# The down projection by seven products instead of eight, in 16 blocks of a fused attention and MLP kernel

## The chip, the cores and the metric

The kernel runs on one core of one Trainium2 chip. The metric is the device time of one execution in microseconds (us). TensorE (PE) multiplies matrices into PSUM; VectorE (DVE), ScalarE (ACT) and GpSimd (POOL) do elementwise work; SyncE (SP) and ACT issue the transfers.

## The reference

One transformer layer for 2048 tokens of width 576: conditioned layer norm, attention over the last 512 keys of a cache with 32 query heads, and an MLP, each with a gated residual. What matters here is the MLP:

```python
gate = jnp.einsum("bsd,df->bsf", x, W_gate)       # 576 -> 4608
up = jnp.einsum("bsd,df->bsf", x, W_up)
gate = gate * (gate > 0)
h = gate * up
return jnp.einsum("bsf,fd->bsd", h, W_down)       # 4608 -> 576
...
h = _layernorm(x, axis=-1) * (1 + cb) + sb
x = x + gb * _B_ref(h, B_W_gate, B_W_up, B_W_down)
```

All is float32. The kernel gets near float32 accuracy from rounded operands: each operand is split into a high part (`hi`, a rounded copy made by ACT) and a low part (`lo`, the remainder, made by POOL's subtraction), and each product is computed as hi\*hi + hi\*lo + lo\*hi, three matmuls.

## The kernel before

The attention takes the first 1640 us or so. Then comes the MLP, in 36 blocks. Blocks m = 0 to 17 (`NFP` is 18) handle the first 1024 tokens, blocks 18 to 35 the second 1024. One block covers 256 of the 4608 hidden features (two tiles of 128, index f) and 1024 tokens (two halves of 512, index k).

Gate and up projection: a block's 2x2 arrangement (f, k) is computed by a seven-product (Strassen-Winograd) scheme. `order(m)` gives the seven slots P1, P6, P2, P7, P5, P4, P3. In each slot `prod` runs twice (xx = 0 gate, xx = 1 up), 7 matmuls of 512 columns each time, into a pair of PSUM banks `gu`; three such pairs rotate. `evac` then takes the result out: in P1 ACT copies it, in P6 and P7 DVE adds a 1024-wide tile, in P2, P5, P4 and P3 DVE finishes one of the four (f, k) tiles of h with two or three instructions (`gated`), and `h_out` splits it: ACT writes `hhi`, POOL writes `hlo`.

Down projection: while block m computes its gate and up products, `md_piece` computes the down product of block m - 1, one piece for each token tile of 128: 2 column halves x 2 feature tiles x 3 = 12 matmuls of 288 columns into the PSUM tile of pool `psW`, which has one buffer, and one DVE addition into the accumulator `acc[i]` in SBUF. `mlp_slots` places the eight pieces of a block among the half slots: slot 0 has one behind its second `prod`, slot 1 one behind each, slots 2 to 6 one behind the first. The last block's pieces follow at the end with nothing beside them; there they alternate between `psW` and `psS`.

The down weights: in blocks 0 to 17 each pair of 128 rows is loaded raw (`rogb`), multiplied by the gate row on DVE, split by ACT and POOL into `wogb`, used, and stored in its split form to memory (`dk`, 576 KB). In blocks 18 to 35 the split form is loaded again. The gate and up operands (`wop`, from `wk`, 640 KB each) and the normalised tokens (`hop`) are loaded again in the same way there.

The order on PE, DVE, ACT and POOL is the order of the program. SP's queue is ordered by the compiler's scheduler.

Of the kernel before, what the change touches and what calls it, by code (L numbers as in the profile page):

```python
# [25 lines left out]
H2 = D // 2  # L26
# [7 lines left out]
def kernel(  # L34
# [13 lines left out]
    nc = tc.nc  # L48
# [182 lines left out]
    mods = {}  # L231
# [183 lines left out]
    qhi, qlo, pthi, ptlo, ohi, olo = {}, {}, {}, {}, {}, {}  # L415
# [25 lines left out]
    st_, t4, t5, pt, hi_, lo_, bc, rb, rinv, ks_, pvps, done, o, bps = ({} for _ in range(14))  # L441
# [192 lines left out]
    NFP = NFT // 2  # L634
    NB = 2 * NFP
    ds_, hhi, hlo = {}, {}, {}
    wop, wraw, hop = {}, {}, {}
    pair, tmp = {}, {}

    def md_piece(m, k, qt, pool=None):  # L640
        b, fp = divmod(m, NFP)
        i = 8 * b + 4 * k + qt
        down_piece([hhi[m, f, k] for f in range(2)], [hlo[m, f, k] for f in range(2)],
                   [ds_[m, f] for f in range(2)], i, qt, f"md{m}_{k}_{qt}", pool=pool)()
        if fp == NFP - 1:
            nc.sync.dma_start(out[i * P:(i + 1) * P, :], acc[i])
# [5 lines left out]
    def order(m):  # L652
        return ("P1", "P6", "P2", "P7", "P5", "P4", "P3")
# [265 lines left out]
    def prod(m, s, n, xx):  # L919

        hs, w = hop[m // NFP, OPS[s][1]], wop[n]
        ps = pair[m, s][:, xx, :]
        ops = []
        for t in range(2):
            ops += [(w[:, xx, t, :], hs[t]), (w[:, xx, 3 + t, :], hs[t]), (w[:, xx, t, :], hs[3 + t])]
        ops.append((w[0:96, xx, 2, :], hs[2][0:96]))
        for i, (a, c) in enumerate(ops):
            nc.tensor.matmul(ps, a, c, start=s not in ("P2", "P3") and i == 0, stop=i == len(ops) - 1,  # L928
                             skip_group_check=True)

    HI = {(0, 0): (op, "ohi"), (1, 0): (op, "ohi"), (1, 1): (bp, "bc"), (0, 1): (bp, "bc")}

    def h_out(m, f, k, r):
        pool, tag = HI[f, k]
# [8 lines left out]
        nc.scalar.copy(hi, r)  # L943
        nc.gpsimd.tensor_sub(lo, r, hi.bitcast(F32))  # L944

    def gated(m, f, k, ps, r, a, op1=ALU.add):

        if a is None:
            nc.vector.tensor_scalar(r, ps[:, 0, :], 0.0, None, op0=ALU.max)
        else:  # L950
            nc.vector.tensor_tensor(r, ps[:, 0, :], a[:, 0, :], op=ALU.add)  # L951
            nc.vector.tensor_tensor(ps[:, 1, :], ps[:, 1, :], a[:, 1, :], op=op1)  # L952
        nc.vector.scalar_tensor_tensor(r, r, 0.0, ps[:, 1, :], op0=ALU.max, op1=ALU.mult)  # L953
        h_out(m, f, k, r)
# [9 lines left out]
    def new_pair(m, s):  # L964
        pair[m, s], kind[m, s] = new_banks(f"gu{npair[0]}")

    def evac(m, s):
        ps = pair[m, s]
        if s == "P1":
            t = tmp["q"] = pp.tile([P, 2, 512], F32, tag="hi", name=f"q{m}")  # L970
            nc.scalar.copy(t, ps)
        elif s == "P2":
            gated(m, 0, 0, ps, xp.tile([P, 640], F32, tag="xm", name=f"r{m}")[:, :512], None)
        elif s == "P6":
            nc.vector.tensor_tensor(tmp["q"], ps, tmp["q"], op=ALU.add)  # L975
        elif s == "P7":
            t = tmp["r"] = pp.tile([P, 2, 512], F32, tag="lo", name=f"r{m}", bufs=2)
            nc.vector.tensor_tensor(t, ps, tmp["q"], op=ALU.add)
            nc.scalar.copy(tmp["q"][:, 1, :], ps[:, 1, :])
        elif s == "P5":  # L980
            t = pp.tile([P, 2, 512], F32, tag="lo", name=f"c22_{m}", bufs=2)
            gated(m, 1, 1, ps, t[:, 0, :], tmp["r"])
        elif s == "P4":
            gated(m, 1, 0, ps, tmp["r"][:, 0, :], tmp["r"])
        else:

            gated(m, 0, 1, ps, tmp["q"][:, 0, :], tmp["q"], ALU.subtract)

    def wd_prep(m, f):
        tag = "wB" if f else "wC"  # L990
        k = 2 * (m % NFP) + f
        if m < NFP:
            load, gate, cut = prep_out(ds_, k, wd, "gb", (m, f), (None, tag))

            def keep():
                cut()
                stores.append((dkeep[k], ds_[m, f][2]))

            return load, gate, keep

        def back():
# [194 lines left out]
    for i, ab in enumerate(lay0 + lay):  # L1196
        n = i - len(lay0) - 2 * NFT + 4
# [4 lines left out]
    def mat(m, s, fn, sums=False):  # L1202
        mextra.setdefault((m, s, sums) if s < 6 else (m + 1, -1, sums), []).append(fn)

    for m in range(NB):
        for f in range(2):
            for k, fn in enumerate(wd_prep(m, f)):
                if m >= NFP:
                    at_ = m, 3 * f
                elif f and m:  # L1210
                    at_ = ((m - 1, 5), (m, 0), (m, 1))[k]
                else:
                    at_ = m, k + (k > 0 and m > 0) + 2 * f
                mat(*at_, fn, sums=k == 1)
# [25 lines left out]

    def mlp_slots():
        for m in range(NB):
            md = [lambda k=k, qt=qt: md_piece(m - 1, k, qt) for k in range(2) for qt in range(4)] if m else []
            for i, s in enumerate(order(m)):
                flush_stores()
                if s not in ("P2", "P3"):
                    new_pair(m, s)
                else:
                    pair[m, s], kind[m, s] = (x[m, {"P2": "P1", "P3": "P5"}[s]] for x in (pair, kind))
                prod(m, s, 7 * m + i, 0)  # L1250
                if m or i:
                    sums(m, i)
                    others(m, i)
                if m and i:
                    md.pop(0)()
                elif filler and not m:
                    filler.pop(0)()
                for fn in mextra.pop((m, i - 1, True), []):
                    fn()
                prod(m, s, 7 * m + i, 1)  # L1260
# [12 lines left out]
        flush_stores()  # L1273
        assert not mextra and not filler
# [204 lines left out]
```

## Time and profile before

| | us |
|---|---|
| median of the runs | 2948.91 |
| lowest and highest run | 2943.78 and 2950.67 |
| the profiled execution's own span | 2950.2 |
| its granted TensorE clock, mean | 0.994 |

The page gives no other time for the profiled execution than its span; it lies within the runs, 1.3 above their median. Of the span PE is busy 2880.4 us, DVE 2103.5, POOL 1870.3 and ACT 1364.6. In the page's groups, `L583` is the line of the down product's matmuls (`md`; the attention's output product shares it as `wo`), `L594` the addition into the accumulator, `L928` the gate and up matmuls (`gu`), `L943` and `L944` the two halves of `h_out`. A row of a timeline gives start, length, engine, line, operation, the tile written and those read, and in brackets the idle time of the engine before it and what ended it. A row of a group gives the count, the busy time, the mean length in ns, and the idle time before. A stretch gives the busy time of each engine in that part of the span, with the number of instructions, then the granted clock and the share of time that transfers filled.

### The profile page before, as it was taken

To read this page: it belongs to the slowest core of one execution; us is meant where nothing else is said; L and a number is where in the kernel's file an instruction comes from. 1 tells how busy PE (TensorE), PEld (TensorE's weight loads), DVE (VectorE), ACT (ScalarE), POOL (GpSimd) and SP (SyncE) were. 2 spreads that over 40 slices of the span, in tenths; PEclk is the share of its full clock that TensorE was granted. 3 is DMA by queue.
4 is the path that set the end of the run, shared out by engine and by line. 5 is a ranking of instruction groups with operands and counts; after the bars stand their busy time and mean duration, and the time that the engine had idled before them with its cause. 6 is when DMAs were issued, how large, how long until landed. Compare 5 with 4: busy or idle time off the path is not lost. (4 is left out here: it accounts for less than half of the span.)

```text
span 2950.2 us, 41160 instructions
## 1 busy us (share of the span) xinstructions
PE 2880.4 (98%) x15406; PEld 2514.2 (85%) x15406; DVE 2103.5 (71%) x2916; ACT 1364.6 (46%) x1869; POOL 1870.3 (63%) x1308
## 2 busy tenths in 40 slices
PE   6799999999999999999999999999999999999999
PEld 5688888888888888888888788888888888888888
DVE  7878888788888888777889676677677444444444
ACT  4466666666676666666656343333333111111110
POOL 5588888888888888777787667777777111111111
PEclk9899999999999999999999999999999999999999
DMA  4011222222323223322244477776777854555443
GB/s 149 22 44 54 82 93 84 67 96 95 98 86 100 92 66 128 101 68 83 70 142 142 138 253 252 267 268 254 264 259 282 285 166 161 168 174 167 158 166 112
DMA packets 167303, 424.75 MB, mean 144 GB/s; under 512 B 15424, under 2 KB 62272, under 8 KB 167104
## 3 DMA queue, kind: packets, MB, share of 16 engines
q1 hardware_dynamic: 131472, 291.58, 31.1%
q10 hardware_dynamic: 35632, 130.53, 11.1%
q8 instruction: 122, 2.00, 0.3%
q14 instruction: 77, 0.63, 0.1%
HBM read 278.17 MB, written 172.20 MB: 153 GB/s over the span
## 5 line engine op out<-in xcount | busy, mean ns | idle before, releaser
L538 POOL TENSOR_TENSOR lo<-p,hi 128x1024 fp32r<-128x1024 f32 x256 | 609.7, 2404 | 0.8 <-ACT hi L518 0.8
L547 POOL TENSOR_TENSOR ks<-ks,p 128x512 f32<-128x512 f32 x256 | 343.6, 1342 | 274.3 <-ACT p L531 207.7
L594 DVE TENSOR_TENSOR acc<-md,acc 128x576 f32<-128x576 f32 x288 | 217.6, 756 | 404.4 <-PE md L583 403.7
L583 PE MATMUL md<-wogb,hhi 128*128 128x288 f32 x2304 | 470.1, 297 | 7.8 <-DVE acc L594 7.8
L459 DVE TRANSPOSE_TENSOR_REDUCE t<-s 128x32 f32<-128x1024 f32 x256 | 316.7, 1244 | 137.7 <-PE s L456 126.4
L583 PEld LDWEIGHTS md<-wogb,hhi 128*128 128x128 f32 x2304 | 385.4, 189 | 33.0 <-DVE acc L594 11.7
L928 PE MATMUL gu<-hop_B,wop 128*128 128x512 f32 (+1 forms) x1512 | 371.8, 393 | 0.4 <-DMA wop<-wk_P 0.3
L583 PE MATMUL md<-wogb,hlo 128*128 128x288 f32 x1152 | 340.5, 296 | 0.0
L944 POOL TENSOR_TENSOR hlo<-r,hhi 128x512 fp32r<-128x512 f32 x72 | 97.8, 1359 | 376.1 <-issue 241.2
L928 PEld LDWEIGHTS gu<-hop_B,wop 128*128 128x128 f32 (+1 forms) x1512 | 278.6, 188 | 55.2 <-ACT lflh L913 0.9
L382 PE MATMUL qps<-hTa,wA 128*128 128x512 f32 x1288 | 312.2, 394 | 9.3 <-ACT lfa L364 7.8
L928 PE MATMUL gu<-hop_T,wop 128*128 128x512 f32 (+1 forms) x1260 | 315.2, 394 | 2.2 <-DMA wop<-wk_P 2.2
L583 PE MATMUL wo<-woga,ohi 128*128 128x288 f32 x1472 | 306.1, 301 | 1.5 <-DVE lfa L362 1.5
L382 PEld LDWEIGHTS qps<-hTa,wA 128*128 128x128 f32 x1288 | 244.5, 190 | 61.6 <-ACT lfa L364 8.2
L529 DVE TENSOR_TENSOR p<-s,mb 128x1024 f32<-128x1024 f32 x246 | 290.2, 1219 | 4.1
L518 ACT CAST hi<-p 128x1024 fp32r<-128x1024 f32 x256 | 269.0, 1051 | 7.1
L928 PEld LDWEIGHTS gu<-hop_T,wop 128*128 128x128 f32 (+1 forms) x1260 | 232.8, 190 | 46.1 <-issue 2.4
L531 ACT ACTIVATE p<-p 128x1024 f32<-128x1024 f32 x246 | 259.8, 1056 | 7.9 <-DVE p L529 7.9
L943 ACT CAST hhi<-r 128x512 fp32r<-128x512 f32 x72 | 44.7, 621 | 447.2 <-DVE r L953 443.9
L583 PEld LDWEIGHTS wo<-woga,ohi 128*128 128x128 f32 x1472 | 238.9, 188 | 9.1 <-issue 1.9
L434 ACT ACTIVATE qhi<-qps 128x512 fp32r<-128x512 f32 x128 | 76.5, 597 | 342.3 <-PE qps L382 342.3
L583 PE MATMUL wo<-woga,olo 128*128 128x288 f32 x736 | 217.2, 295 | 0.3 <-POOL olo L572 0.2
(205 smaller groups left out, 6290.8 us busy)
## 6 DMA issues: line engine op xcount, KB each, us to landing
wop<-wk_P SPq DMA_DIRECT2D x133, 640.0 KB
wk_P<-wop ACTq DMA_DIRECT2D x119, 640.0 KB
wr<-wlay SPq DMA_DIRECT2D x68, 384.0 KB
dk<-wogb ACTq DMA_DIRECT2D x36, 576.0 KB
wogb<-dk SPq DMA_DIRECT2D x36, 576.0 KB
againq<-akq SPq DMA_DIRECT2D x18, 640.0 KB
rogb<-wd SPq DMA_DIRECT2D x36, 288.0 KB
rwA<-wq SPq DMA_DIRECT2D x32, 320.0 KB
```

Of the source, the lines that this page charges most:

```text
L382: return [lambda i=i, a=a, b=b: nc.tensor.matmul(ps, a, b, start=(i == 0), stop=(i == n - 1)) for i, (a, b) in enumerate(ops)]
L434: nc.scalar.activation(qhi[u], qst[u][0], AF.Copy, bias=0.0, scale=SCALE)
L459: nc.vector.tensor_reduce(t4[u][:, 2 * h:2 * h + 2, :].rearrange("p k b -> p (k b)"), t.rearrange("p k (b j) -> p (k b) j", j=32), axis=AX ...
L518: nc.scalar.copy(hi_[u, h], pt[u, h])
L529: nc.vector.tensor_tensor(p, t, bc[u][:, None, :].to_broadcast([P, 2, 512]), op=ALU.subtract)
L531: nc.scalar.activation(p, p, AF.Exp, bias=0.0, scale=1.0)
L538: nc.gpsimd.tensor_sub(lo_[u, h], pt[u, h], hi_[u, h].bitcast(F32))
L547: nc.gpsimd.tensor_tensor(ks_[u], ks_[u], p[:, j, :], op=ALU.add)
L583: nc.tensor.matmul(ps[:, half, :H2], a[:, sl], w[b][:, cs], start=(n == 0 and seed is None), stop=(n == 5), skip_group_check=seed is not None)
L594: nc.vector.tensor_tensor(av, ps[:, :, :H2], av, op=ALU.add)
L928: nc.tensor.matmul(ps, a, c, start=s not in ("P2", "P3") and i == 0, stop=i == len(ops) - 1, skip_group_check=True)
L944: nc.gpsimd.tensor_sub(lo, r, hi.bitcast(F32))
```

## The change

In blocks 19 to 34 (`ST`) the down product is computed by the same seven-product scheme on the 2x2 arrangement (token half, feature tile) x (feature tile, column half): four tiles of h and four quarters of the weights are combined into seven operands each (A and S; B and T), and seven products of 512 x 128 x 288 replace eight. A product is done in two pieces (q) of 256 tokens: 2 token tiles x 3 = 6 matmuls of 288 columns. There are 14 pieces, two in each slot, of the following block. P2, P4 and P3 go on accumulating in the PSUM tile of the piece before them (`second`), after DVE has read it. Each piece is followed by one DVE addition of 576 columns, into an accumulator or into the sum `su`, which keeps P1 + P6 over all 16 blocks and is added to the accumulators at the end (`st_end`).

The operands of h are split by ACT and POOL as they come (`st_cut`); DVE makes the four sums S1 to S4 in the next block's slots 0 to 2 (`st_sums`). The weights are loaded raw (`sw_load`, slot 0), multiplied by the gate row on POOL (`sw_gate`, slot 2), combined on POOL (`sw_sum`) and split by ACT and POOL in seven parts of 288 columns (`sw_cut`, slots 3, 4, 6 and 0 of the next block). The split weights of these blocks are no longer stored in the first half nor loaded again. Block 35's reload moves to slot 2. Accumulators are paired in one tile (`accp`), and tiles of the finished first half hold raw operands.

```diff
+    accp = [res.tile([P, 2, D], F32, tag=f"accp{i}", name=f"acc{i}") for i in range(S // (2 * P))]
     for i in range(S // P):
-        acc.append(res.tile([P, D], F32, name=f"acc{i}"))
+        acc.append(accp[i // 2][:, i % 2, :])
...
+    ST = range(NFP + 1, NB - 1)
+    STP = {"P1": ("A11", "B11"), "P2": ("A12", "B21"), "P3": ("S4", "B22"), "P4": ("A22", "T4"),
+           "P5": ("S1", "T1"), "P6": ("S2", "T2"), "P7": ("S3", "T3")}
...
+    def st_cut(m, key, raw):
...
+        nc.scalar.copy(hi, raw)
+        nc.gpsimd.tensor_sub(lo, raw, hi.bitcast(F32))
+
+    def st_sums(m, which):
+        a11, a12, a21, a22 = (st_raw(m, *STA[k]) for k in ("A11", "A12", "A21", "A22"))
+        for key in which:
+            out, a, b, o = {"S1": (a22, a21, a22, ALU.add), "S3": (a21, a11, a21, ALU.subtract),
+                            "S2": (a11, a22, a11, ALU.subtract), "S4": (a12, a12, a11, ALU.subtract)}[key]
+            nc.vector.tensor_tensor(out, a, b, op=o)
+            st_cut(m, key, out)
+
+    def sw_load(m):
+        for f in range(2):
+            sraw[m, f] = rp.tile([P, 640], F32, tag="raw", name=f"rogb{m}_{f}")[:, :D]
+            nc.sync.dma_start(sraw[m, f], wd[2 * (m - NFP) + f])
+
+    def sw_gate(m):
+        for f in range(2):
+            nc.gpsimd.tensor_tensor(sraw[m, f], sraw[m, f], mods["gb"], op=ALU.mult)
...
+    def sw_prep(m, i):
+        if i == 2:
+            sw_gate(m)
+        elif i == 3:
+            for key in ("T3", "T1", "T2"):
+                sw_sum(m, key)
+            sw_cut(m, "B11")
+            sw_cut(m, "B21")
+        elif i == 4:
+            sw_sum(m, "T4")
+            sw_cut(m, "T3")
+            sw_cut(m, "T4")
+        elif i == 6:
+            sw_cut(m, "T1")
+            sw_cut(m, "B22")
+
+    def st_tile(m, p, q, st):
+        a, b = STP[p]
+        (hi, lo), w = sh[m, a], sw[m, b]
+        second = p in ("P2", "P4", "P3")
+        if not second:
+            st["ps"] = psW.tile([P, 2, 512], F32, tag="w", name=f"st{m}_{p}_{q}")
+        ps = st["ps"]
+        for j in range(2):
+            sl = slice((2 * q + j) * P, (2 * q + j + 1) * P)
+            for n, (x, y) in enumerate(((hi, 0), (hi, 1), (lo, 0))):
+                nc.tensor.matmul(ps[:, j, :H2], x[:, sl], w[:, y, :], start=n == 0 and not second, stop=n == 2,
+                                 skip_group_check=True)
...
+            nc.vector.tensor_tensor(t, ps[:, :, :H2], t, op=ALU.add)
+
+    def st_list(m):
+        st = {}
+        return [lambda p=p, q=q: st_tile(m, p, q, st)
+                for a, b in (("P1", "P2"), ("P7", "P4"), ("P5", "P3"), ("P6", None)) for q in range(2)
+                for p in (a, b) if p]
+
+    def st_end(k, q):
+        u = held["u"][:, 2 * q:2 * q + 2, :]
+        for h in range(1 - k, 2):
+            t = accp[4 + 2 * k + q][:, :, h * H2:(h + 1) * H2]
+            nc.vector.tensor_tensor(t, t, u, op=ALU.add)
...
-                stores.append((dkeep[k], ds_[m, f][2]))
+                if m + NFP not in ST:
+                    stores.append((dkeep[k], ds_[m, f][2]))
...
-                    at_ = m, 3 * f
+                    at_ = m, 2 if m > NFP else 3 * f
...
+            two = m - 1 in ST
+            if two:
+                md = st_list(m - 1)
...
+                if m in ST and i == 0:
+                    sw_load(m)
-                if m and i:
+                if two or m and i:
                     md.pop(0)()
...
+                if two and i == 0:
+                    if m - 1 in ST:
+                        sw_cut(m - 1, "T2")
+                if two and i < 3:
+                    st_sums(m - 1, (("S1", "S3"), ("S2",), ("S4",))[i])
+                if m in ST:
+                    sw_prep(m, i)
                 prod(m, s, 7 * m + i, 1)
                 wop.pop(7 * m + i)
-                if m and i < 2:
+                if two or m and i < 2:
                     md.pop(0)()
...
         for k in range(2):
             for qt in range(4):
+                if qt % 2 == 0:
+                    st_end(k, qt // 2)
                 md_piece(NB - 1, k, qt, (psS, "s") if qt % 2 else None)
```

More of the change, by code (lines that the diff above doesn't have):

```diff
@@ new lines, in st_cut @@
+    def st_cut(m, key, raw):
+        if key in ("A11", "A22", "A12"):
+            hi = op.tile([P, 512], F32R, tag="ohi", name=f"sh{m}_{key}")
+            lo = op.tile([P, 512], F32R, tag="olo", name=f"sl{m}_{key}")
+        elif key == "S2":
+            hi, lo = (bp.tile([P, 512], F32R, tag="bc", name=f"s{x}{m}_{key}") for x in "hl")
+        else:
+            t = pp.tile([P, 2, 512], F32R, tag="p", name=f"sh{m}_{key}")
+            hi, lo = t[:, 0, :], t[:, 1, :]
+        sh[m, key] = hi, lo
+        nc.scalar.copy(hi, raw)
+        nc.gpsimd.tensor_sub(lo, raw, hi.bitcast(F32))
@@ new lines, in sw_gate, with sw_sum @@
+    def sw_gate(m):
+        for f in range(2):
+            nc.gpsimd.tensor_tensor(sraw[m, f], sraw[m, f], mods["gb"], op=ALU.mult)
+    def sw_sum(m, key):
+        b11, b12, b21, b22 = (sraw[m, f][:, h * H2:(h + 1) * H2] for f in range(2) for h in range(2))
+        if key == "T3":
+            sraw[m, "x"] = xp.tile([P, 640], F32, tag="xm", name=f"sx{m}")
+        t3, t2 = sraw[m, "x"][:, :H2], sraw[m, "x"][:, H2:D]
+        out, a, b = {"T3": (t3, b22, b12), "T1": (b12, b12, b11), "T2": (t2, b22, b12), "T4": (b21, b21, t2)}[key]
+        nc.gpsimd.tensor_tensor(out, a, b, op=ALU.subtract)
+        sraw[m, key] = out
@@ new lines, in sw_cut @@
+    def sw_cut(m, key):
+        if key == "T2":
+            w = res.tile([P, 2, H2], F32R, tag="accp3", name=f"sw{m}_{key}")
+        elif key in ("B11", "T3", "T1"):
+            sw["t"] = wp.tile([P, 2, 2, H2], F32R, tag="wC", name=f"sw{m}_{key}")
+            w = sw["t"][:, 0]
+        else:
+            w = sw["t"][:, 1]
+        raw = {"B11": sraw[m, 0][:, :H2], "B21": sraw[m, 1][:, :H2], "B22": sraw[m, 1][:, H2:]}
+        raw = raw[key] if key in raw else sraw[m, key]
+        sw[m, key] = w
+        nc.scalar.copy(w[:, 0, :], raw)
+        nc.gpsimd.tensor_sub(w[:, 1, :], raw, w[:, 0, :].bitcast(F32))
@@ L972, in evac @@
         elif s == "P2":
-            gated(m, 0, 0, ps, xp.tile([P, 640], F32, tag="xm", name=f"r{m}")[:, :512], None)
+            gated(m, 0, 0, ps, st_raw(m, 0, 0) if m in ST else
+                  xp.tile([P, 640], F32, tag="xm", name=f"r{m}")[:, :512], None)
         elif s == "P6":
@@ L980, in evac @@
         elif s == "P5":
[L981 to L982 removed]
+            t = (st_raw(m, 1, 1) if m in ST else
+                 pp.tile([P, 2, 512], F32, tag="lo", name=f"c22_{m}", bufs=2)[:, 0, :])
+            gated(m, 1, 1, ps, t, tmp["r"])
         elif s == "P4":
[L984 removed]
+            gated(m, 1, 0, ps, st_raw(m, 1, 0) if m in ST else tmp["r"][:, 0, :], tmp["r"])
         else:
[L987 removed]
+            gated(m, 0, 1, ps, st_raw(m, 0, 1) if m in ST else tmp["q"][:, 0, :], tmp["q"], ALU.subtract)
     def wd_prep(m, f):
@@ L1242, in mlp_slots @@
         for m in range(NB):
-            md = [lambda k=k, qt=qt: md_piece(m - 1, k, qt) for k in range(2) for qt in range(4)] if m else []
+            two = m - 1 in ST
+            if two:
+                md = st_list(m - 1)
+            else:
+                md = [lambda k=k, qt=qt: md_piece(m - 1, k, qt) for k in range(2) for qt in range(4)] if m else []
             for i, s in enumerate(order(m)):
```

25 lines of the change are left out of this document (added).

## The prediction

> **What bounds the kernel now.** I read the page's head first, then the table by stretches, then the chain of waits in order of time. Its columns are start, length and work.
>
> ```profile
> span 2950.2 us, 41160 instructions
> ...
> core 0: us, PE busy (x) PEld busy (x) DVE busy (x) ACT busy (x) POOL busy (x), PEclk, DMA share, GB/s
> 2352.00:2387.00 35.00, 35.00 (x194) 30.97 (x194) 16.02 (x21) 3.81 (x7) 5.18 (x4) 1.00 0.48 162
> 2107.00:2142.00 35.00, 34.59 (x192) 30.37 (x191) 25.24 (x28) 11.50 (x16) 28.81 (x25) 1.00 0.76 263
> 2282.00:2317.00 35.00, 32.45 (x170) 28.08 (x169) 14.05 (x19) 5.26 (x8) 7.41 (x7) 0.95 1.03 353
> ```
>
> ```profile
> 2330.63 1.60 PE md L583 x12
> 2332.23 4.83 PE gu L928 x21
> ...
> 2367.51 4.83 PE gu L928 x21
> ...
> 2402.79 4.83 PE gu L928 x21
> ...
> 2933.59 12.81 PE md L583 x96
> ```
>
> In the second token half PE is busy all 35.00 us of a stretch, at clock 1.00, and the chain holds nothing but its two lines. The three 4.83 rows stand 35.28 apart: that is one block, 98 gate/up matmuls (gu) and 96 down matmuls (md). Twelve md take 1.60, so one is 0.133; the tail's 96 in 12.81 agree. DVE, ACT and POOL have more than half of the block free. Removed md matmuls therefore shorten the run until something else makes PE wait. The span is 1.3 above the runs' median of 2948.9; I subtract from the median.
>
> **The change, part by part.** (1) Matmuls. A block's down product was 8 pieces of 12; it becomes 14 pieces of 6, that is 84. 16 blocks x 12 x 0.133 = 25.6 us less PE work; the block becomes 35.28 - 1.60 = 33.68, if PE never waits.
>
> (2) PSUM handover. All pieces still use the one psW buffer, so each waits until DVE has added the one before into SBUF. There are now two pieces in each of the seven slots: 7 gu (1.60), piece (0.80), 7 gu (1.60), piece (0.80). The slot's own evacuation stands on DVE behind the second piece's add, and the next slot's first add stands behind that evacuation. First PE, then DVE, ACT and POOL by time:
>
> ```profile
> 2662.41 1.76 PE L928 MATMUL gu<-hop_B,wop 128*128 128x512 f32 x7
> 2664.01 0.43 PE L583 MATMUL md<-wogb,hhi 128*128 128x288 f32 x2
> ...
> 2662.61 0.76 DVE L594 TENSOR_TENSOR acc<-md,acc 128x576 f32<-128x576 f32 x1 [2.44 <-PE md L583]
> 2663.28 1.22 DVE L975 TENSOR_TENSOR q<-gu,q 128x1024 f32<-128x1024 f32 x1
> ...
> 2651.39 0.69 DVE L951 TENSOR_TENSOR q<-gu,q 128x512 f32<-128x512 f32 x1 [0.85 <-PE gu L928]
> 2652.18 0.70 DVE L952 TENSOR_TENSOR gu<-gu,q 128x512 f32<-128x512 f32 x1
> 2652.92 0.69 DVE L953 SCALAR_TENSOR_TENSOR q<-q,gu 128x512 f32<-128x512 f32 x1
> ...
> 1958.66 0.69 DVE L953 SCALAR_TENSOR_TENSOR c<-c,gu 128x512 f32<-128x512 f32 x1
> 1959.27 5.33 DVE L734 TENSOR_TENSOR wr<-wr,wr 128x768 f32<-128x768 f32 x1
> ...
> 2653.72 0.62 ACT L943 CAST hhi<-q 128x512 fp32r<-128x512 f32 x1 [4.29 <-DVE q L953]
> ...
> 2654.41 1.29 POOL L944 TENSOR_TENSOR hlo<-q,hhi 128x512 fp32r<-128x512 f32 x1 [3.61 <-ACT hhi L943]
> ```
>
> ```profile
> 2254.45 0.68 DVE acc L594
> 2255.13 0.04 issue
> 2255.18 1.86 PE md L583 x12
> ```
>
> Let E be the start of the matmul after a slot's second piece. The add starts 0.20 later (2662.41 to 2662.61); the next DVE instruction 0.67 after it (2663.28); the three gated instructions follow at 0.79 and 0.74, and what comes next at 0.61 (1958.66 to 1959.27). So the next slot's first add starts at E+3.01 and ends at E+3.77. Its second piece is due at E + 1.60 + 0.80 + 1.60 = E+4.00. When PE really waits (last fence) it starts 0.05 after the add and the piece takes 1.86 for 1.60; 0.17 of that is the overlap between rows (the 1.76 row, whose follower starts after 1.60), 0.09 is loss. So the add must end 0.14 early, by E+3.86: it fits by 0.09. This tight spot comes three times a block, after the slots of P5, P4 and P3; elsewhere the evacuation is at most 1.4 us and the spare is 0.8 or more. I take 0, the row arithmetic's answer; the other end is a rival.
>
> (3) Sums on DVE: four a block (S1, S3, S2, S4), both inputs in SBUF.
>
> ```profile
> 1959.18 0.72 POOL L705 TENSOR_TENSOR wop<-wr,wop 32x256 fp32r<-32x256 f32 x1 [1.83 <-ACT wop L704]
> 1959.88 1.28 POOL L706 TENSOR_TENSOR wop<-wr,wop 128x512 fp32r<-128x512 f32 x1
> 1961.12 1.41 POOL L181 TENSOR_TENSOR wogb<-rogb,wogb 128x576 fp32r<-128x576 f32 x1
> 1962.50 1.27 POOL L944 TENSOR_TENSOR hlo<-c,hhi 128x512 fp32r<-128x512 f32 x1
> ...
> 1239.04 0.67 DVE L544 TENSOR_TENSOR ks<-p 128x512 f32<-128x512 f32 x1
> ```
>
> ```profile
> L594 DVE TENSOR_TENSOR acc<-md,acc 128x576 f32<-128x576 f32 x136 | 103.0, 757 | 246.8 <-PE md L583 246.8
> L944 POOL TENSOR_TENSOR hlo<-r,hhi 128x512 fp32r<-128x512 f32 x35 | 45.3, 1294 | 301.0 <-issue 241.2 <-ACT hhi L943 59.8
> L943 ACT CAST hhi<-r 128x512 fp32r<-128x512 f32 x34 | 21.1, 621 | 297.4 <-DVE r L953 297.4
> ...
> L181 POOL TENSOR_TENSOR wogb<-rogb,wogb 128x576 fp32r<-128x576 f32 x36 | 51.1, 1420 | 0.0
> ...
> L180 ACT CAST wogb<-rogb 128x576 fp32r<-128x576 f32 x36 | 24.1, 670 | 0.0
> ```
>
> Alone such a sum takes 0.67 (1239.04); one begun under a POOL run took 5.33, until the four POOL rows had ended (1962.50 + 1.27 = 1963.77). Adds that read PSUM don't show this. The Trainium skill (SBUF — State Buffer, "SBUF: two separate sides") gives the rule: a DVE instruction with two SBUF inputs and a GpSimd instruction exclude each other for a whole instruction. By it alone a sum would wait one POOL instruction at most; the trace shows a whole run, and I go by the trace.
>
> So I place POOL's work from E, the start of slot 0. In the slot before, P4's gated result is ready at -4.80 + 3.09 = -1.7. ACT rounds A12 at -1.6 (0.62), POOL subtracts it from -0.9 to 0.4 (1.29), then the low parts of T1, B22 and T2. A 288-wide POOL instruction is an estimate, on the line through 1294 and 1420: 0.84. POOL is free at 2.9. S1 follows slot 0's first add, at 3.01 + 0.67 = 3.7, S3 at 4.4; ACT rounds S1 only when it is done, so POOL starts again at 5.1. S1's and S3's low parts end at 7.7; S2 follows slot 1's first add, at 4.80 + 2.60 + 0.67 = 8.1; S4 stands ahead of POOL's long run of slots 2 and 3 in program order. All four sums fall in gaps: cost 0, spares of 0.8 (S1) and 0.4 (S2, behind which DVE has nothing due until slot 1's second piece ends at 9.6). After S1 and S3, DVE is free at 5.0, just when slot 0's second add falls due (4.80 + 0.20); it ends at 5.8, and slot 1's first piece needs it by 4.80 + 1.60 - 0.14 = 6.3: 0.5 to spare.
>
> (4) Rest of the added work, per block. DVE: 16.0 + 6 x 0.757 + 4 x 0.67 = 23.2 of 33.7. POOL: 7 x 1.29, two gate multiplies of 1.42 and eleven 288-wide instructions = 21.1, before 5.2. ACT: three casts of 0.62 and seven of about 0.45 more, 3.8 + 5.0 = 8.8. The split operands are needed one to four slots after they are made; the nearest is A12's low part, done at 0.4 and used at 4.0. PE covers all of it; should that cover fail, it shows as PE waiting for POOL.
>
> (5) DMA.
>
> ```profile
> dk<-wogb ACTq DMA_DIRECT2D x36, 576.0 KB
> wogb<-dk SPq DMA_DIRECT2D x36, 576.0 KB
> rogb<-wd SPq DMA_DIRECT2D x36, 288.0 KB
> ...
> by line: PE gu L928 19.8%; PE md L583 12.0%; DVE wr L734 1.1%; DMA wop<-wk_P 0.5%; issue 0.5%; POOL wop L706 0.4%; DMA hx_T<-hb 0.2%; DVE acc L594 0.2%; DMA hk_T<-hx_T 0.2%; POOL wop L705 0.1%; DVE q L975 0.1%; DVE gu L952 0.1%; DVE c L951
> ```
>
> 32 of the dk stores and 32 of their reloads go, 32 raw loads of half the size come; in the second half transfers fill 0.48 of the time, so nothing is lost there. On SP the two raw loads wait for POOL's last reads of the buffers (E+1.2, E+2.1); the wop loads queued behind them wait for PE until about E+3.2 anyhow. Block 35's two reloads move from slots 0 and 3 to slot 2 and have four slots, some 19 us, to land. In the first half the stores leave ACT's queue and the 0.76-full transfers. PE loses 0.41 us in 2107:2142 and 2.55 in 2282:2317. What the reordering does there can't be read off: its waits are the lock of (3), 1.1% of the chain or 32 us. A fifth of that, 6 us, either way is my bound; I take 0.
>
> (6) Tail. Six SBUF adds (0.75 each, an estimate: 0.67 x 576/512) stand before the last pieces. The add of the first piece starts at 3.01 + 0.75 and ends at 4.5; the third piece, due at E+3.20, waits for psW: +1.3 us. Later ones catch up. The accumulators paired in one tile move no instruction; the raw operands kept in finished accumulators wait for output stores issued a block earlier: 0.
>
> Sum: 2948.9 - 25.6 + 1.3 = **2924.6**.
>
> **Rivals.** A, handovers late: if DVE's queue runs 0.2 to 0.4 longer than the rows say (by waits on two semaphores, for instance), 48 handovers lose 0.11 to 0.31 each: 5 to 15 us, so 2930 to 2939. For: the spare is 0.09. Against: I used the slowest of the three gated sets. B, slower, by the lock: if S1 finds POOL in a run, DVE stands, the adds behind it are late, and PE waits for psW in the same slot. A hold like 1959.27's, 4.5 until 1963.77, less the 0.5 of slack, is 4.0 a block: 16 x (4.0 - 1.6) + 1.3 = +40, so 2989. It turns to a loss when the hold passes 2.1 us, that is when POOL's run into slot 0 ends after E+5.8 instead of 2.9. For: POOL's work grows fourfold. Against: the gap of 0.8 and the in-order start of the next run. C, clock: many short PE pauses drop the granted clock. The trace gave 0.95 in 2282:2317, where PE lost 2.55 us; at 0.95 through 16 blocks of 33.7 it costs 27 us: 2952. Against: 2107:2142 lost 0.41 and kept 1.00. The Trainium skill (TensorE: Matmul & The Clock Gate, "A second HAM failure mode: psum-queue depth-cycling") describes such a fall, to half the clock, for cycling PSUM buffers; no stretch quoted here shows it for short pauses. D: A's upper end with holds of some 0.5 us a block beyond the slack: 2939 + 8 = 2947.
>
> **How the numbers follow.** Forecast 0.58 (2915 to 2931: the first half's 6 us either way, and 3.5 more at the low end, half of what the runs differ by), A 0.22, D 0.08, B 0.10, C 0.02. A measurement of this kernel tells about 0.2% (5.9 us) from no change. Faster: forecast, A and a little of D, 0.81; same: the rest of D, and C, 0.09; slower: B, 0.10. The range 2915 to 2940 takes in forecast and A and leaves 0.2 out.
>
> **What would show it.** Right: gated rounds 33.7 apart in blocks 20 to 35, PE busy throughout, DVE near 23 and POOL near 21 us a block, sums at 0.67. A: PE waiting for the adds of slots 0, 5, 6. B: sums of several us ending with a POOL run. Wrong altogether: PE waiting for POOL's low parts or for weights.

## The result, and the profile after

| | before | changed |
|---|---|---|
| median of the runs, us | 2949.79 (4 runs, 2943.78 to 2950.98) | 2932.05 (4 runs, 2927.97 to 2935.76) |
| ratio | | 0.9947, 95% interval 0.9933 to 0.9962 |
| the profiled execution's span, us | 2950.2 | 2926.2 |
| its granted TensorE clock, mean | 0.994 | 0.996 |

The changed kernel is faster by 17.7 us, or 0.5%, and the interval leaves no change out. The forecast was 2924.6 and a gain of 24.3: the direction and the range hold, and the gain falls 6.6 us short. The profiled pair differs by 24.0, but it flatters the change, as the experiments on the first half show below.

The head of the page of the changed kernel, and its table by stretches (length; busy time of PE, PEld, DVE, ACT and POOL with the number of instructions; granted clock; DMA share; GB/s):

```profile
span 2926.2 us, 41388 instructions
```

```profile
2404.00:2439.00 35.00, 35.00 (x190) 30.65 (x189) 22.51 (x32) 8.48 (x16) 21.24 (x21) 1.00 0.46 155
2439.00:2474.00 35.00, 35.00 (x187) 30.49 (x187) 23.26 (x33) 8.48 (x16) 20.29 (x20) 1.00 0.47 151
2107.00:2142.00 35.00, 35.00 (x195) 30.99 (x194) 26.17 (x27) 11.23 (x16) 27.63 (x25) 1.00 0.63 226
2282.00:2317.00 35.00, 33.09 (x183) 28.64 (x182) 13.95 (x19) 4.08 (x6) 6.34 (x5) 1.00 1.04 386
```

In the two stretches of the second half PE is still busy all the time at clock 1.00, DVE has 22.5 to 23.3 us of work, POOL 20.3 to 21.2 and ACT 8.5 beside it. That is the picture that the prediction drew. What it did not draw is in the chain of waits (start, length, work):

```profile
2642.13 0.81 PE st_P L1030 x6
2642.93 1.62 PE gu L929 x7
2644.56 0.81 PE st_P L1030 x6
2645.37 1.62 PE gu L929 x7
```

There is no wait in it. But 7 gate/up matmuls take 1.62 instead of 1.60, and 6 down matmuls 0.81 instead of 0.80. The length of a block can be read from ACT's one large copy a block, of which this view of one line gives the first and the last start; the first row is the kernel before, the second the changed one:

```profile
L971 ACT COPY q<-gu x14: 1015/1015/1015, 2442.9 to 2901.6; 128x1024 f32<-128x1024 f32 x14
```

```profile
L1095 ACT COPY q<-gu x14: 1006/1007/1008, 2436.9 to 2879.4; 128x1024 f32<-128x1024 f32 x14
```

Thirteen blocks took 458.7 us before and take 442.5 now: 35.28 and 34.04 a block. The forecast was 33.68. 16 x (35.28 - 34.04) is 19.8 us, less 1.7 that the tail lost (below): 18.1, which is the difference of the medians within 1 us. So the shortfall is 0.36 us in each of 16 blocks, with PE never waiting: the matmuls stand further apart. About two thirds of it lie in the gate/up matmuls, whose operands did not change: by the starts in the two traces they take 22.50 us a block before and 22.74 now.

The handover and the sums, from the timelines of PE, DVE and POOL in slot 0 (start, length, line, work, and in brackets the idle time before and its end):

```profile
2673.60 0.43 PE L1030 MATMUL st_P<-sw_B,sh_A 128*128 128x288 f32 x2
```

```profile
2671.93 0.69 DVE L1077 SCALAR_TENSOR_TENSOR q<-q,gu 128x512 f32<-128x512 f32 x1
2672.54 0.75 DVE L1039 TENSOR_TENSOR su<-st_P,su 128x576 f32<-128x576 f32 x1
2673.21 0.68 DVE L969 TENSOR_TENSOR srb<-q,srb 128x512 f32<-128x512 f32 x1
2673.92 0.69 DVE L969 TENSOR_TENSOR q<-sra,q 128x512 f32<-128x512 f32 x1
2674.61 0.76 DVE L1039 TENSOR_TENSOR acc<-st_P,acc 128x576 f32<-128x576 f32 x1
```

```profile
2669.66 1.58 POOL L1002 TENSOR_TENSOR sw_T<-rogb,sw_T 128x288 fp32r<-128x288 f32 x2
2671.20 0.81 POOL L1002 TENSOR_TENSOR sw_T<-sx,sw_T 128x288 fp32r<-128x288 f32 x1
2674.62 1.29 POOL L962 TENSOR_TENSOR sh_S<-srb,sh_S 128x512 fp32r<-128x512 f32 x1 [2.61 <-ACT sh_S L961]
```

The first add ends at 2673.29, and the piece that waits for it starts at 2673.60: on time by 0.31, of which 0.14 are needed. S1 and S3 take 0.68 and 0.69, in the gap between POOL's 2672.01 and 2674.62. All of this is where the prediction had put it, within some tenths of a us.

The tail, by PE's waits:

```profile
PE md L584 <- issue: 0.9, 1, 0.9
PE md L584 <- DVE acc L595: 0.2, 1, 0.2
```

This view shows two waits, 1.1 in all, where 1.3 was forecast; but it leaves out the time by which rows overlap. By the starts of the matmuls the first piece of the tail begins 1.06 after its turn and the third 0.35 after its own, and from the last product's piece to the last matmul it takes 1.7 us more than the same matmuls would without a wait.

### The profile page after: what moved, and what is told of

It is laid out like the page before. It is cut to its first block, busy times and chain, and to the rows that moved or that the text cites. A ratio compares the mean times of both kernels' runs of the same rounds, so it can differ in the third digit from the quotient of the medians.

```text
span 2926.2 us, 41388 instructions
## 1 busy us (share of the span) xinstructions
PE 2854.1 (98%) x15214; PEld 2483.7 (85%) x15214; DVE 2220.3 (76%) x3082; ACT 1432.2 (49%) x2029; POOL 2110.1 (72%) x1564
## 5 line engine op out<-in xcount | busy, mean ns | idle before, releaser
L929 PE MATMUL gu<-hop_B,wop 128*128 128x512 f32 (+1 forms) x1512 | 378.2, 393 | 0.0
L584 PE MATMUL md<-wogb,hhi 128*128 128x288 f32 x1280 | 261.8, 297 | 9.6 <-DVE acc L595 8.7
L595 DVE TENSOR_TENSOR acc<-md,acc 128x576 f32<-128x576 f32 x160 | 120.5, 754 | 152.6 <-PE md L584 151.5
L584 PEld LDWEIGHTS md<-wogb,hhi 128*128 128x128 f32 x1280 | 212.8, 188 | 24.8 <-DVE acc L595 12.7
L1039 DVE TENSOR_TENSOR acc<-st_P,acc 128x576 f32<-128x576 f32 x160 | 120.9, 756 | 133.8 <-PE st_P L1030 133.8
L584 PE MATMUL md<-wogb,hlo 128*128 128x288 f32 x640 | 188.9, 295 | 0.0
L573 POOL TENSOR_TENSOR olo<-rb,ohi 128x512 fp32r<-128x512 f32 x128 | 166.6, 1302 | 23.7 <-ACT ohi L569 23.2
```

What stands on the lines that cost most here:

```text
L573: nc.gpsimd.tensor_sub(olo[u], o.pop(u), ohi[u].bitcast(F32))
L584: nc.tensor.matmul(ps[:, half, :H2], a[:, sl], w[b][:, cs], start=(n == 0 and seed is None), stop=(n == 5), skip_group_check=seed is not None)
L1039: nc.vector.tensor_tensor(t, ps[:, :, :H2], t, op=ALU.add)
```

## The experiments

**What sets the slower spacing: order, waits, traffic?** And has the first half gained?

The changed kernel once more:

> The changed kernel once more, as it stands, beside the next two on one chip. Its first two profiles gave a block of 34.03 us in blocks 20 to 35 where 33.68 was forecast, no wait of PE there, and a span shorter by 24.0 in the profiled pair while the medians differ by 17.7. If the block is what the change is worth, the medians settle at 16 x (34.03 - 35.28) + 1.4 for the tail = -18.6, about 2931; if the first half has gained as well, nearer to -24, about 2926.

Measured: 2931.42 (5 runs, 2931.28 to 2935.66), ratio 0.9943, interval 0.9931 to 0.9955. Its block is again 34.04. The gain is 17.6, about what the blocks and the tail give, and not the 24.0 of the profiled pair.

The stores of the first half put back:

```diff
-                if m + NFP not in ST:
-                    stores.append((dkeep[k], ds_[m, f][2]))
+                stores.append((dkeep[k], ds_[m, f][2]))
```

> The changed kernel, but the first half still stores all 36 split weight pairs to DRAM as the kernel before does, 32 of them for nobody. This gives the first half its old transfers back and leaves the second as it is. If the first half gained from the stores that went, this costs up to 6 us against the changed kernel (2932 to 2938), and the time from the first gate/up matmul to block 20 is longer by as much; if they were hidden, it is within 0.1% of it.

Measured: 2927.04 (6 runs, 2924.74 to 2937.44), ratio 0.9932, interval 0.9918 to 0.9947: not slower. From ACT's copy of block 0 to that of block 18 it takes 652.4 us, the changed kernel 653.7 and 657.0 in its two profiles, and the kernel before 655.5 (worked out from the start times in the traces). These stores were hidden, and the stretch varies by more than they could bring. Over the fourteen profiles of this case it lies between 652.4 and 657.5, so this stretch alone can make two runs of one kernel differ by several us.

The pieces in pairs:

```diff
-            st["ps"] = psW.tile([P, 2, 512], F32, tag="w", name=f"st{m}_{p}_{q}")
+            pool, tag = (px["x"], "x") if q else (psW, "w")
+            st[q] = pool.tile([P, 2, 512], F32, tag=tag, name=f"st{m}_{p}_{q}")
...
-                for a, b in (("P1", "P2"), ("P7", "P4"), ("P5", "P3"), ("P6", None)) for q in range(2)
-                for p in (a, b) if p]
+                for p in ("P1", "P2", "P7", "P4", "P5", "P3", "P6") for q in range(2)]
...
+                    free.remove("x")
...
-                if two or m and i:
+                if m and i and not two:
                     md.pop(0)()
...
+                if two:
+                    md.pop(0)()
```

> The same products, but the two pieces of a slot run one behind the other after 14 gate/up matmuls, and they use two PSUM buffers in turn (the third gate/up pair is given up for the second one); the products go in the order P1, P2, P7, P4, P5, P3, P6. So PE's order is 14 and 12 again, as before the change, with the 84 matmuls of the change. Theory 1, the alternation of 7 and 6 sets the slower spacing: 7 gate/up fall back from 1.625 to 1.603 us, 6 down from 0.807 to 0.799, the block to 33.7, the time by 5.4 us below the changed kernel. Theory 2, waits for DVE's adds set it: there are as many waits as in the changed kernel, so the block stays near 34.0, or lies between, as each add now has more room. Theory 3, the added work of ACT, POOL and the transfers beside PE sets it: block 34.0, no change. The rival against the edit itself: with two gate/up pairs a new pair waits for an evacuation of 2.9 us, 0.6 more than the pieces behind it take, so PE would wait and the block would come out longer than 34.0.

```profile
L1095 ACT COPY q<-gu x14: 1009/1010/1010, 2436.7 to 2876.5; 128x1024 f32<-128x1024 f32 x14
```

A block of 33.83 (439.8 over 13), between the two numbers; in time 2929.74 (5 runs, 2925.41 to 2936.36), ratio 0.9941, not to be told from the changed kernel. The two gate/up pairs sufficed: PE never waits in these blocks, so the rival against the edit falls. The order takes part, but it does not explain everything.

Then four kernels that tell order, waits and traffic apart. Before's own down product in pieces of 6 (first fence) and of 12 (second), one token tile of eight left out:

```diff
+            cut = m - 1 in range(NFP + 1, NB - 1)
+            if cut:
+                md = [lambda k=k, qt=qt, h=h: md_half(m - 1, k, qt, h) for k in range(2) for qt in range(4)
+                      for h in range(2)][:14]
```

> The kernel before the change, with its own down product in blocks 19 to 34, but cut into pieces of one column half: 6 matmuls each, 14 pieces a block, two a slot as in the changed kernel. Of the 16 half pieces two are left out in each of these blocks, that is one of the eight 128-token tiles. There are no sums, no splitting of weights and no raw loads in it, and the operands are those of before. Theory 1 (the alternation of 7 and 6 sets the spacing, by itself): block 34.03 as in the changed kernel, 7 gate/up 1.625 us, 6 down 0.807. Theory 3 (the added work of ACT, POOL and the transfers): 33.69, with 1.603 and 0.799. The pair kernel has put 0.20 of the 0.35 us to the order; a split verdict would be 33.83 to 33.9 here.

```profile
L982 ACT COPY q<-gu x14: 1014/1015/1016, 2438.1 to 2876.7; 128x1024 f32<-128x1024 f32 x14
```

```profile
2621.20 0.81 PE md L656 x6
2622.01 1.60 PE gu L939 x7
2623.61 0.80 PE md L656 x6
2624.40 1.61 PE gu L939 x7
```

```diff
+            if cut:
+                md.pop()
```

> As the last one, the same eighth of the down product left out in blocks 19 to 34, but in whole pieces of 12, one in each slot, 14 gate/up matmuls between them: before's order with one piece less, and 7 adds instead of 14. All theories but one give 33.68 (35.28 less 12 x 0.133), the block that was forecast; if it comes out at 34.0, the sum 12 x 0.133 itself was wrong and neither order nor traffic is the cause.

```profile
L971 ACT COPY q<-gu x14: 1015/1015/1016, 2431.8 to 2869.9; 128x1024 f32<-128x1024 f32 x14
```

Pieces of 12 give 33.70 (438.1 over 13): the sum 12 x 0.133 was right for before's matmuls. Pieces of 6 in the order of the changed kernel give 33.74 (438.6): the alternation costs 0.04, not 0.35, and theory 1 falls. The chain of the 6-matmul kernel shows something else: its pieces take 0.81 and 0.80 in turn, and 7 gate/up 1.61 and 1.60.

The adds left out, except those of product 6:

```diff
+        if p != "P6":
+            return
-        if p == "P1" and m == ST[0]:
+        if m == ST[0]:
```

> The changed kernel with DVE's adds of the pieces left out, except those of product 6 (so most products are computed and dropped): PE never waits for DVE before a piece that follows an add left out, and DVE's two long queues are gone. PE's instructions and their order are those of the changed kernel, 7 and 6 in turn. Theory 2 (the waits on DVE's adds slow the spacing): block 33.7 to 33.8. Theories 1 and 3: 34.0, as in the changed kernel.

```profile
L1097 ACT COPY q<-gu x14: 1006/1006/1006, 2439.9 to 2882.8; 128x1024 f32<-128x1024 f32 x14
```

One block's split weights for 16 blocks:

```diff
-        (hi, lo), w = sh[m, a], sw[m, b]
+        (hi, lo), w = sh[m, a], sw[ST[0], b]
...
-                if m in ST and i == 0:
+                if m == ST[0] and i == 0:
                     sw_load(m)
...
-                if m in ST:
+                if m == ST[0]:
                     sw_prep(m, i)
```

> The changed kernel, but the raw down weights are loaded, gated, summed and split for block 19 alone, and the products of the other 15 blocks use block 19's (their own weights are left out of the result). POOL's work falls from 20 to about 9 us a block and ACT's from 8.5 to about 5, and the raw loads go. Theory 3 (that traffic beside PE slows the spacing): block 33.7 to 33.85. Theory 1: 34.0. Waits for operands: PE waits for ACT's and POOL's splits in the changed kernel and not here, so a fall could also be those waits; the no-add kernel beside it tells whether waits count at all.

```profile
L1095 ACT COPY q<-gu x14: 1002/1008/1010, 2442.0 to 2884.5; 128x1024 f32<-128x1024 f32 x14
```

34.07 (442.9) and 34.04 (442.5): with 12 of DVE's 14 adds gone, and with most of POOL's and about half of ACT's new work gone, the spacing is that of the changed kernel. Theories 2 and 3 fall. The granted clock is 1.00 from 2440 to 2870 us in the traces of these runs, as in those before and after the change, so it is not the clock either.

**Where a piece writes, or what it reads?** What was left on PE were two differences: the changed kernel's pieces write two PSUM banks, and they read other operands. First before's operands with pieces over two banks (two token tiles j, one feature tile f), shown against the 6-matmul kernel:

```diff
-                nc.tensor.matmul(ps[:, h, :H2], a[:, sl], ds_[m, f][b][:, cs], start=n == 0, stop=n == 5)
+                nc.tensor.matmul(ps[:, j, :H2], a[:, sl], ds_[m, f][b][:, cs], start=n == 0, stop=n == 2)
```

> The 6-matmul kernel (before's own down product in half pieces, an eighth of it left out, no sums or splits) came to a block of 33.74, the changed kernel to 34.03, with the same count and order of matmuls; waits for adds and the work of the other engines are out. What still differs on PE is where a piece writes: in the 6-matmul kernel all six matmuls of a piece write one PSUM bank (one token tile, one column half, both feature tiles); in the changed kernel three write one bank and three the other (two token tiles, one feature tile). This kernel cuts before's down product in the second way: two token tiles, three matmuls each, one feature tile, again 14 of 16 pieces a block (an eighth left out). Theory 4 (the change of bank in the middle of a piece slows the spacing): block 34.0, 7 gate/up 1.624, 6 down 0.807. Rival (something in the operands or the program of the changed kernel, such as where its split operands lie): 33.74 as in the 6-matmul kernel.

```profile
L982 ACT COPY q<-gu x14: 1015/1015/1017, 2439.1 to 2878.0; 128x1024 f32<-128x1024 f32 x14
```

```profile
2600.66 0.80 PE md L656 x6
...
2603.07 0.79 PE md L656 x6
...
2605.47 0.79 PE md L656 x6
...
2607.88 0.79 PE md L656 x6
```

Then the changed kernel's operands with pieces in one bank:

```diff
-                nc.tensor.matmul(ps[:, j, :H2], x[:, sl], w[:, y, :], start=n == 0 and not second, stop=n == 2,
+                nc.tensor.matmul(ps[:, 0, 224 * j:224 * j + H2], x[:, sl], w[:, y, :], start=n == 0 and not second, stop=n == 2,
...
+        t, r = t[:, :, :256], ps[:, 0, :].rearrange("p (a n) -> p a n", a=2)
```

> The other direction: the changed kernel, but both token tiles of a piece write into one PSUM bank, the second one 224 columns behind the first, so that they overlap in 64 columns; DVE adds 256 columns of each instead of 288 (the last 32 columns of each half and the overlapped ones are not the reference's). PE's matmuls, their sizes, their order and their operands stay. Theory 4 (change of bank): block 33.74, 7 gate/up 1.609, 6 down 0.801. Rival (operands or program): 34.03.

```profile
L1096 ACT COPY q<-gu x14: 1007/1010/1010, 2439.3 to 2882.1; 128x1024 f32<-128x1024 f32 x14
```

33.76 (438.9) for two banks with before's operands, 34.06 (442.8) for one bank with the changed kernel's: theory 4 falls in both directions, and the operands remain. The two-bank kernel also says which property of them. By the distances between the starts of its matmuls in the trace, its pieces take 0.795, 0.791, 0.790 and 0.789 one after another (the four rows of its chain), then 0.803 twice, then 0.795 and 0.791, and go on in twos. Its pieces read column half 0 twice, then half 1 twice, and at the border of two blocks half 0 comes four times. So the shorter pieces are those of column half 0. In the changed kernel each split weight lies in two parts of 288 columns, one behind the other: the high part stands where a half 0 would, the low part 1152 bytes on, where a half 1 would. Every piece reads both, and every piece takes 0.807.

This was tried by the layout alone:

```diff
-            w = res.tile([P, 2, H2], F32R, tag="accp3", name=f"sw{m}_{key}")
+            w = res.tile([P, 2, 2, H2], F32R, tag="accp3", name=f"sw{m}_{key}")[:, :, 0]
...
-            w = sw["t"][:, 0]
+            w = sw["t"][:, :, 0]
...
-            w = sw["t"][:, 1]
+            w = sw["t"][:, :, 1]
```

> The changed kernel with another layout of its split weights, and nothing else: in the tile that holds the parts of two operands, and in that of T2, the low part lies 2304 bytes behind the high part, as in the kernel before, instead of 1152; the second operand begins at 1152. Why: the two-bank kernel came to 33.77 (the change of bank is out), the one-bank kernel to 34.07, and in their rows the pieces go by the column half that they read. In the 6-matmul kernel the pieces of column half 0 take 0.795 and those of half 1, 1152 bytes further on, 0.807, in turn, with 1.616 and 1.602 before them; in the two-bank kernel two fast pieces follow two slow ones, as the halves do there. In the changed kernel high and low part are 1152 apart, so every piece reads from both kinds of place, and every piece takes 0.807 and every 7 gate/up 1.626. Theory 5 (where the moving operand begins, in steps of 1152 bytes, sets the spacing): here each piece reads from one kind of place, the first product of a pair from the one and the second from the other, as the 6-matmul kernel does, so block 33.74, pieces of 0.795 and 0.807 in turn, and 4.6 us less than the changed kernel in all, about 2927. Rival (anything else in the split operands or their program): 34.03 and pieces of 0.807 throughout.

```profile
L1095 ACT COPY q<-gu x14: 1002/1006/1008, 2442.8 to 2881.3; 128x1024 f32<-128x1024 f32 x14
```

```profile
2625.25 1.60 PE gu L929 x7
2626.86 0.80 PE st_P L1030 x6
2627.65 1.61 PE gu L929 x7
2629.27 0.81 PE st_P L1030 x6
```

The block is 33.73 (438.5 over 13), as the 6-matmul kernel's, and the pieces take 0.80 and 0.81 in turn. The time is 2924.94 (5 runs, 2923.91 to 2929.85), ratio 0.9913, interval 0.9900 to 0.9927, below the interval of the changed kernel: a version that beats both. The layout of the split weights is the cause of 0.31 of the 0.36.

Theory 5 stands in part. Counted with the seven gate/up matmuls behind it, a piece costs the same from either kind of place while the two take turns: by the starts in this trace it is 0.795 + 1.616 = 2.411 from the one and 0.806 + 1.603 = 2.409 from the other. A piece of the changed kernel, which reads from both, comes to 0.807 + 1.624 = 2.431 on average, and 14 times the difference of 0.021 is the 0.30 that a block gained by the starts. So what costs is that one piece reads from both kinds of place, and two thirds of the cost fall on the gate/up matmuls behind it. All parts on the place of the shorter pieces would, as an estimate, bring little more: in the two-bank kernel, where such pieces also follow each other, the second of two comes to 2.408 with its gate/up matmuls (the second of two from the other place to 2.420). Why the mixture costs, and which step of the address counts, no run here shows.

**The two rivals of the prediction, made to happen.** The adds of slot 0 later by one instruction:

```diff
+            if m in ST:
+                nc.vector.tensor_tensor(st_raw(m, 1, 0), ps[:, 0, :], tmp["r"][:, 0, :], op=ALU.add)
             gated(m, 1, 0, ps, st_raw(m, 1, 0) if m in ST else tmp["r"][:, 0, :], tmp["r"])
```

> The prediction's rival A made to happen at one of its three places: in the gated evacuation of P4 DVE does its first instruction twice (the same values, 0.69 us more), so that the adds of the next slot 0 come 0.69 later. In the changed kernel the tightest add ended 0.31 before its piece; a waiting piece starts 0.05 after the add and 0.09 goes into a late weight load, so the spare is 0.17 and PE loses about 0.5 a block: 34.5, with PE waiting for the piece's add once a block. If the handover has more room than the rows say, the block stays at 34.0.

```profile
L1095 ACT COPY q<-gu x14: 1005/1009/1010, 2439.8 to 2888.3; 128x1024 f32<-128x1024 f32 x14
```

```profile
PE st_P L1030 <- DVE su L1039: 2.9, 12, 0.2
```

34.50 (448.5 over 13): 0.69 more on DVE costs 0.46, so the spare at this place was 0.23 (0.17 expected), and PE waits for exactly that add, once a block.

POOL's run in slot 0 longer by seven instructions:

```diff
                         sw_cut(m - 1, "T2")
+                        for _ in range(7):
+                            t2 = sw[m - 1, "T2"]
+                            nc.gpsimd.tensor_sub(t2[:, 1, :], sraw[m - 1, "T2"], t2[:, 0, :].bitcast(F32))
```

> The prediction's rival B made to happen: in slot 0 POOL writes the low part of T2 seven more times (the same values), so that its run goes on until 5.7 us later, to 5.0 us or so past the start of the sum S1 on DVE, which reads two SBUF operands. By the trace (DVE L734 held 5.33 us under four POOL instructions) S1 is held until the whole run ends, about 4.5 us; 2.1 of that are slack, so PE loses 2.4 a block and the block comes to about 36.4 (35.9 to 36.9). By a wait for one POOL instruction only, S1 is held 0.8 at most and the block stays at 34.0.

```profile
L1095 ACT COPY q<-gu x14: 1002/1005/1009, 2441.7 to 2895.7; 128x1024 f32<-128x1024 f32 x14
```

```profile
2683.20 1.13 DVE L969 TENSOR_TENSOR srb<-q,srb 128x512 f32<-128x512 f32 x1
2684.37 1.19 DVE L969 TENSOR_TENSOR q<-sra,q 128x512 f32<-128x512 f32 x1
```

```profile
2682.09 7.31 POOL L1401 TENSOR_TENSOR sw_T<-sx,sw_T 128x288 fp32r<-128x288 f32 x7
2689.36 1.30 POOL L962 TENSOR_TENSOR sh_S<-srb,sh_S 128x512 fp32r<-128x512 f32 x1
```

```profile
PE st_P L1030 <- POOL sh_S L962: 4.1, 13, 0.3
```

34.92 (454.0): neither 36.4 nor 34.0. DVE's and POOL's timelines of one slot 0 (the first two fences) and PE's waits (the last): S1 starts in the middle of POOL's run and takes 1.13, S3 1.19, instead of 0.68 and 0.69. They are held 0.45 and 0.50, not until the run ends at 2689.40. POOL is held in turn: its seven take 7.31 instead of 7 x 0.81. The sum S2 starts in a gap between two of the seven, at 2688.05, and takes 0.68: it is not held. The Trainium skill (SBUF — State Buffer, "SBUF: two separate sides") has this exclusion last for one instruction, and here the trace agrees. The 0.9 that a block lost have two sources: slot 0's second add, behind two held sums, comes late, so that the piece behind it starts 0.3 late (the rows below), and the low parts of S1 and S3, queued behind POOL's longer run, come so late that PE waits for POOL (the row above).

```profile
2685.48 0.74 DVE L1039 TENSOR_TENSOR acc<-st_P,acc 128x576 f32<-128x576 f32 x1
```

```profile
2684.38 1.76 PE L929 MATMUL gu<-hop_T,wop 128*128 128x512 f32 x7
2686.28 0.54 PE L1030 MATMUL st_P<-sw_B,sh_A 128*128 128x288 f32 x2
```

The row of 5.33 us in the prediction differs from this run in its gaps. There the four POOL rows overlap at their ends (1959.18 + 0.72 is later than 1959.88), while the seven here start 0.08 after each other's ends. The trace of the kernel before shows that this decides: of its 68 sums of that line (L734), 43 began under a POOL row and ended 0.82 after the end of the first POOL row that the next one did not overlap. That row was the one under which the sum began 21 times, and otherwise the second to fourth of a chain; a gap of 0.055 was enough to let the sum in. Only four sums got in between two rows that overlapped. So this run tried rival B with the kind of POOL run that holds a sum least. In the changed kernel POOL's own low parts in slot 0 do overlap (2669.66 + 1.58 is later than 2671.20), and what a sum that begins under those would lose was not tried.

## Why the prediction was right or wrong, point by point

- **The bound and the matmul count**: PE is the bound before and after, and removing 12 matmuls of before's kind is worth what the sum said (33.70 in the kernel with pieces of 12). This step was right, and with it the direction.
- **Term (1), -25.6**: mis-sized; it measured -19.8. The step that failed is "the block becomes 35.28 - 1.60 = 33.68, if PE never waits". PE never waited, and the block was 34.04. The step took the distance between matmuls from before's rows, gave it to matmuls that read from another layout, and left the gate/up matmuls at their old distance, where two thirds of the shortfall lie. The layout run puts 0.31 of the 0.36 to the place of the low part in the tile; 0.04 the 6-matmul kernel shows with before's own operands, so they belong to the order of 7 and 6.
- **Term (2), the handover at 0**: right, with 0.31 between add and piece at the tightest place, and a spare of 0.23 by the late run where 0.09 was forecast. The measured time lies in the interval of rival A (2930 to 2939), but A's mechanism did not happen: its sign was to be PE waiting for adds, and there is none in blocks 20 to 35. The forecast's own range ended at 2931, just below the measured 2932; that the stated range holds is luck, as it reached to 2940 only for A's sake.
- **Term (3), the sums at 0**: right, at 0.68 and 0.69 in the gap of POOL. The price of rival B, 4.0 a block, stays open: with POOL's instructions 0.08 apart a sum is held 0.45 to 0.50, and what POOL's length costs first is the lateness of its own results; with POOL's rows overlapping, the trace of before shows holds through up to four rows. The prediction read its one long hold rightly, but did not say on what it depends.
- **Term (4), the loads of DVE, POOL and ACT**: right (22.5 to 23.3, 20.3 to 21.2, 8.5; a POOL instruction of 288 columns took 0.81 where 0.84 was estimated), and the work stayed covered by PE; taking most of POOL's new work and about half of ACT's away did not change the block.
- **Term (5), the first half at 0**: right as far as can be told. Putting the stores back did not make it slower. The bound of 6 us either way is about the spread of that stretch from run to run (652.4 to 657.5).
- **Term (6), the tail at +1.3**: right in kind, 1.7 by the starts. PE waits behind DVE's queue, as forecast, but the larger part (1.06) stands before the first piece, which needs psW from the last product's add; the sum had the wait at the third piece alone.
- **Clock (rival C)**: 1.00 in both stretches of the second half; it did not happen.

## What to carry to other kernels

When PE is the bound and never waits, the rest of the time is in the distance between matmuls, and a per cent of it is larger than most waits that one looks for: read the length of a group of matmuls before and after, and of the group behind it too, not only the busy share, which is full in both. A scheme that saves products but stores its operands in a new layout should first keep the old distances between parts, as that cost nothing here: it was worth 0.31 us a block, a quarter of what the change brought. And a median difference explained to within 1 us by one steady stage is a better measure than the span of one profiled pair.

## What the runs showed of the hardware that was not expected

Six matmuls of 288 columns and the seven gate/up matmuls behind them, the same in number, size and order, take 2.41 or 2.43 us together, depending on where the operand of 288 columns (the split weights, the moving operand of the texts above) lies in SBUF: 2.41 when the two parts that a piece reads lie 2304 bytes apart, 2.43 when they lie 1152 apart. The length of one group alone misleads: a piece takes 0.795 from one kind of place and 0.806 from the other, but the seven behind it take 1.616 and 1.603, so the sum is the same.

A piece that starts late, right behind its add, is followed by a faster group: behind the tightest piece of slot 0 the seven gate/up matmuls take 1.603 instead of 1.626 (from the starts in the trace of the changed kernel). In the kernel without the adds no group is faster (1.625 or 1.626 throughout), and in the late run the group behind the waiting piece takes 1.606 on average. So a wait of some hundredths there is partly given back; why, no run shows.

A DVE sum of two SBUF operands that begins under a POOL instruction waits until POOL leaves a gap: where POOL's instructions stood 0.08 apart it took 0.45 to 0.50 us longer, and where four overlapped the longest took 5.40 us instead of 0.95.
